# Attention and two expert layers on one core: where the weighted sums of a unit stand among its steps

## The chip, the cores and the metric

The kernel runs on one core of a Trainium2 chip. The metric is the device time of one execution in microseconds (us). The engines are named as in the profile: PE (TensorE, matrix multiplications), PEld (its weight loads), DVE (VectorE), ACT (ScalarE), POOL (GpSimd) and SP (SyncE, which issues the transfers).

## The reference, cut to what matters

```
scores = scale * np.matmul(q, k.transpose(0, 1, 3, 2))        # q, k, v: 4 x 8 x 576 x 64
...
scores = scores + bias.transpose(2, 0, 1)[None, :, :, :]
scores = scores - np.max(scores, axis=-1, keepdims=True)
attn = np.exp(scores)
attn = attn / (np.sum(attn, axis=-1, keepdims=True) + 1e-09)
return np.matmul(attn, v).astype(np.float32)
```

Attention over 4 batches of 8 heads, 576 positions each, 64 wide, with a bias that a small network makes from positions. Behind it come a layer with eight experts, one of which is chosen for each token, and a gated feed-forward layer. The change touches the attention alone, and in it the last line above: the sum of the values weighted by the attention.

## The kernel before, in words

The bias is made first and put into DRAM. Then the attention runs through 16 units; a unit is one batch and one pair of heads (`units`, with index `ui`). A unit has five steps, c = 0 to 4. In steps 0 to 3 the scores of 128 queries against all 576 keys are computed for each of the two heads (`s_pe`, L251); step 4 is the tails' step: the last 64 queries of both heads share the 128 rows. All of it is emitted by one loop over `steps`, whose index is n = 5 ui + c, under a manual schedule: each engine does its instructions in the order in which the code is written.

A step n emits in this order:

- the first half of the transposes of the tile of two steps ago (`t_pe` with i = 0, L274: eight transposes into two PSUM tiles T, four into each), and their copies out of PSUM (`t_ev`, on DVE, L281);
- the scores of the present tile (L251, twelve matmuls of 288 columns with 64 rows each, which run in pairs; in step 4 six with 128 rows);
- the second half of the transposes (ten into two T tiles; two where the old tile is a tails' tile), copied out of PSUM by ACT (L279);
- the weighted sums that stand in this step's list `pe[n]`; in step 1, after the first of them, also the transposes that spread the reciprocals of the row sums (`bc_recip`, L316) and four copies by ACT (L323, L324);
- the bias with the running extremum on DVE (`s_max`, L255), the exponential on ACT (L260), what stands in `ve[n]` on DVE, and loads.

`t_tile` gives out the T tiles from a pool with two buffers:

```
def t_tile():
    return pO.tile([128, 512], F32, tag="T", bufs=2, name="T")
```

A half of the transposes takes both of them. So each half can begin only when the half before it has been copied out of PSUM: the first tile's first transpose after the first copy, the second tile's after the second copy.

The weighted sums of a unit (`pv_list`, L336) are ten blocks: five blocks of keys for queries 0 to 255 (256 columns) and five for queries 256 to 575 (320 columns). A block is two matmuls, one for each head, which the trace shows as four instructions. Five blocks of one kind add up in one PSUM tile `pv` (a pool of two buffers), and one operation on DVE takes it out (L342; at steps 5 ui + 7 and 5 ui + 10). In which step the blocks stand is set by two dictionaries: the key is the step counted from the unit's first, the value is how many blocks.

```
PVA = {4: 1, 5: 2, 6: 2}
PVB = {7: 2, 8: 2, 9: 1}
```

Steps 5 to 9 are steps 0 to 4 of the next unit. So in the steady state there are two blocks in each step, and in the tails' step one of 320 columns of the unit before and one of 256 of the present unit. In step 1 the two blocks stand on either side of the reciprocals' transposes, so there are six groups of blocks between other work in a unit.

What is left of the last unit when the loop ends (`pvq`) is put by hand into the code behind it: `pvs(2)` takes two entries of that list, between the last transposes; the rest goes into the first steps of the expert layer (`at(i, ...)` with 2, 2, 2 and 1 entries).

Of the kernel before, what the change touches and what calls it, by code (L numbers as in the profile page):

```python
# [27 lines left out]

PVA = {4: 1, 5: 2, 6: 2}
PVB = {7: 2, 8: 2, 9: 1}
BL = (20, 28, 30, 32, 36)
VL = (7, 12, 13, 14)
LG = (1, 5, 5, 7, 8, 10, 10)
# [73 lines left out]
def body(tc, qt, kt, va, vb, ws, moe_w_gate, moe_w_output_gate, moe_w1, moe_w2, w_gate, w_val, w_out, ctab, cst, cst2, out):  # L109
    nc = tc.nc  # L110
    with ExitStack() as ctx:
# [153 lines left out]
        def t_pe(E, c, i):  # L265

            t = [t_tile() for _ in range(2)]
            ns = ([128 * n for n in range(4)], [128 * n for n in range(4, 9)])[i] if c < 4 else [128 * n for n in range(4)] if i == 0 else [512]  # L270
            for j, n in enumerate(ns):
                for r in range(2):
                    k, o = slice(64 * r, 64 * r + 64), n + (64 * r if c == 4 and i == 0 else 0)
                    nc.tensor.transpose(t[r][:, 64 * j:64 * j + 64], E[k, o:o + 128], ident[k, k])  # L274
            return t
# [7 lines left out]
        def t_ev(p, b, c, t, i):  # L283

            pt = pts[p, b][c // 2 if c < 4 else 1]
            for r in range(2):
                if c < 4:
                    o, n = 128 * (c % 2) + 64 * r, 4 + i
                    copy(i, pt[:, 4 * i:4 * i + n, o:o + 64], t[r][:, 0:64 * n].rearrange("p (n t) -> p n t", n=n))
                elif i == 0:  # L290
                    copy(i, pt[:, 5 * r:5 * r + 4, 256:320], t[r][:, 0:256].rearrange("p (m t) -> p m t", m=4))
                else:
                    k = slice(64 * r, 64 * r + 64)
                    copy(i, pt[k, 4, 256:320], t[r][k, 0:64])
# [31 lines left out]
        def pv_list(p, b, f):  # L326

            st = {}
            res = []
            w = (256, 320)[f]  # L330
            for c in range(5):
                def m(c=c):
                    if c == 0:
                        st["ps"] = pO.tile([128, 512], F32, tag="pv", bufs=2, name="pv")
                    for hh in range(2):
                        nc.tensor.matmul(st["ps"][64 * hh:64 * hh + 64, 0:w], vt[p][:, hh, b, c, :],  # L336
                                         pts[p, b][f][:, c + (5 * hh if c < 4 else 0), :], start=c == 0, stop=c == 4)
                res.append(m)

            def ev():  # L340
                o = 256 * f
                nc.vector.tensor_tensor(xT[p][:, b * S + o:b * S + o + w], st["ps"][:, 0:w], rbs[p, b][:, o:o + w], ALU.mult)  # L342
            return res, ev
# [491 lines left out]
        pe, ve = {}, {}  # L835
# [6 lines left out]
        for n, (ui, c) in enumerate(steps):  # L842
            p, b = units[ui]
            g = 9 * ui + min(2 * c + 1, 8)
            if c == 0:
# [12 lines left out]
                (m0, e0), (m1, e1) = pv_list(p, b, 0), pv_list(p, b, 1)  # L858
                for ms, q in ((m0, PVA), (m1, PVB)):
                    for k, w in q.items():  # L860
# [96 lines left out]


        pvq = [f for n in sorted(pe) for f in pe[n]]
        pvq = pvq[0:4] + [ve[82][0]] + pvq[4:] + [ve[85][0]]  # L960

        def pvs(n):
            for _ in range(n):
                if pvq:
                    pvq.pop(0)()
# [64 lines left out]
        late.pop()()  # L1030
        for f in lows:
            f()
        pvs(2)
        t_ev(*a[0:3], t_pe(a[3], a[2], 1), 1)
        pvs(2)
        t_ev(*z[0:3], t_pe(z[3], z[2], 0), 0)
# [249 lines left out]
```

## Time and profile before

| | us |
|---|---|
| median of three runs | 1046.68 (1044.06 to 1047.58) |
| the profiled execution, its own time | 1044.97 |
| its span, from the first instruction to the last | 1043.2 |
| PE busy in the span | 1000.8 (96%) |
| DVE, ACT, POOL busy | 577.5, 456.8, 117.1 |

The attention's steps run from 67.7 to about 326 us, the expert layer and the feed-forward layer behind it. In the timeline a row is one or several instructions of one line; where rows of one engine overlap, the engine works on them in a pipeline, so what a group of instructions costs is read from its start to the start of what comes behind it, and not from its own length. A row's bracket says how long the engine was idle ahead of it and whose work ended that.

### The profile page before, as it was taken

How to read it: one execution, taken by the hardware profiler on the slowest of the kernel's cores; microseconds unless marked ns; L12 is line 12 of the kernel's file. 1: busy time of each engine (PE TensorE's matmuls, PEld its weight loads, DVE VectorE, ACT ScalarE, POOL GpSimd, SP SyncE). 2: the span in 40 equal slices, each digit the busy share in tenths (PEclk: the TensorE clock that was granted, in tenths of full speed). 3: DMA queues.
4: the chain of work that ended last, by engine and by line, in shares of the span. 5: the costliest groups of instructions: out<-in, count | busy, mean ns of one | idle time of the engine just before them, and what ended most of it. 6: DMA issues, size and time to landing. Idle time of an engine off the chain costs nothing. (4 is left out here: it accounts for less than half of the span.)

```text
span 1043.2 us, 18947 instructions
## 1 busy us (share of the span) xinstructions
PE 1000.8 (96%) x7525; PEld 797.0 (76%) x7525; DVE 577.5 (55%) x1321; ACT 456.8 (44%) x1027; POOL 117.1 (11%) x117
## 2 busy tenths in 40 slices
PE   6979999999999999999999899999999999999998
PEld 2336666666666899998999677778888888888897
DVE  8966767777766644544566599952223223222322
ACT  6766777777766433332435455431113112211221
POOL 2662332342320000000000000000000000000000
PEclk9997999999999999999999999999999999999999
DMA  6774323333103242633724655511002000200010
GB/s 190 207 258 131 94 84 117 107 105 107 36 3 110 65 163 102 239 118 130 264 102 147 200 175 165 177 51 51 1 1 77 5 1 0 61 1 1 17 25 21
DMA packets 67756, 101.91 MB, mean 98 GB/s; under 512 B 9136, under 2 KB 37936, under 8 KB 67664
## 3 DMA queue, kind: packets, MB, share of 16 engines
q1 hardware_dynamic: 67504, 100.41, 30.3%
q8 instruction: 60, 0.98, 0.4%
q14 instruction: 32, 0.26, 0.1%
q10 hardware_dynamic: 160, 0.26, 0.1%
HBM read 74.63 MB, written 26.03 MB: 96 GB/s over the span
## 5 line engine op out<-in xcount | busy, mean ns | idle before, releaser
L1181 PE MATMUL v<-x,w 128*128 128x512 f32 (+1 forms) x720 | 161.2, 371 | 3.8 <-DVE w L934 3.8
L1181 PE MATMUL g<-x,w 128*128 128x512 f32 (+1 forms) x720 | 158.5, 369 | 1.9 <-ACT x L1136 1.9
L1181 PEld LDWEIGHTS v<-x,w 128*128 128x128 f32 x720 | 125.0, 189 | 31.9 <-DVE w L934 7.5
L1181 PEld LDWEIGHTS g<-x,w 128*128 128x128 f32 x720 | 126.7, 188 | 26.6 <-ACT x L1136 2.1
L1203 PE MATMUL o<-w,uh 128*128 128x512 f32 x432 | 133.4, 390 | 0.0
L1184 DVE TENSOR_TENSOR t<-g,t 128x512 f32<-128x512 f32 (+1 forms) x60 | 38.2, 636 | 168.4 <-ACT t L1183 168.4
L260 ACT ACTIVATE E<-E,st 128x576 f32<-128x576 f32 x144 | 110.6, 774 | 6.4 <-DVE st L255 6.0
L274 PEld LDWEIGHTS T<-ident,E 64*128 64x128 f32 x1312 | 65.6, 141 | 55.5 <-ACT pt L279 27.7
L255 DVE CUSTOM_DVE_ANT_0 E<-S,bias 128x576 f32<-128x576 f32 x128 | 91.9, 755 | 17.9 <-PE S L251 9.4
L1183 ACT ACTIVATE t<-g 128x512 f32<-128x512 f32 (+1 forms) x60 | 33.1, 552 | 153.9 <-PE g L1181 153.9
L336 PE MATMUL pv<-pt,rawv 128*64 128x256 f32 (+1 forms) x640 | 99.3, 423 | 0.0
L1188 ACT ACTIVATE uh<-t 128x512 fp32r<-128x512 f32 (+1 forms) x60 | 35.4, 589 | 145.7 <-DVE t L1185 145.7
L274 PE MATMUL T<-ident,E 64*128 64x64 f32 x1312 | 92.2, 238 | 6.2 <-ACT rb L324 3.6
L1203 PEld LDWEIGHTS o<-w,uh 128*128 128x128 f32 x432 | 80.4, 188 | 16.1
L281 DVE COPY pt<-T 128x256 f32<-128x256 f32 x160 | 59.7, 414 | 54.3 <-PE T L274 54.2
L1203 PE MATMUL o<-w,ul 128*128 128x512 f32 x216 | 84.1, 389 | 0.0
L251 PE MATMUL S<-kh,qz 64*128 64x288 f32 (+1 forms) x576 | 77.6, 320 | 5.2 <-DVE st L255 4.6
L279 ACT ACTIVATE pt<-T 128x320 f32<-128x320 f32 (+1 forms) x160 | 56.0, 391 | 54.5 <-PE T L274 52.4
L545 ACT ACTIVATE qz<-T 128x288 fp32r<-128x288 f32 x63 | 25.8, 410 | 105.6 <-PE T L543 105.5
L546 DVE SCALAR_TENSOR_TENSOR qz<-T,qz 128x288 fp32r<-128x288 f32 x63 | 28.7, 456 | 74.2 <-ACT qz L545 73.7
L1185 DVE TENSOR_TENSOR t<-v,t 128x512 f32<-128x512 f32 (+1 forms) x60 | 38.3, 638 | 54.4 <-PE v L1181 53.1
L251 PEld LDWEIGHTS S<-kh,qz 64*128 64x128 f32 (+1 forms) x576 | 54.8, 192 | 8.0 <-DVE st L255 6.0
(242 smaller groups left out, 1643.9 us busy)
## 6 DMA issues: line engine op xcount, KB each, us to landing
raww<-in_moe_w_dram SPq DMA_DIRECT2D x16, 768.0 KB, 6.1
bscr<-ob SPq DMA_DIRECT2D x36, 288.0 KB, 4.0
bias<-bscr SPq DMA_DIRECT2D x16, 576.0 KB, 5.0
rw<-in_w_gate_dram SPq DMA_DIRECT2D x12, 512.0 KB, 3.8
rw<-in_w_val_dram SPq DMA_DIRECT2D x12, 512.0 KB, 3.6
rw<-in_w_out_dram SPq DMA_DIRECT2D x12, 512.0 KB, 4.0
rawq<-in_qt_dram SPq DMA_DIRECT2D x16, 320.0 KB, 3.8
rawk<-in_kt_dram SPq DMA_DIRECT2D x16, 288.0 KB, 3.2
```

The costliest lines, as they stand in the source:

```text
L251: nc.tensor.matmul(t[:, f, 0:288], x[k, a], y[k, o], start=i == 0, stop=i == 2)
L255: nc.vector.tensor_tensor_reduce(out=E.rearrange("p (a b) -> p a b", a=2), in0=ps[:, :, 0:288], in1=bt[p, hh, c].rearrange("p (a b) -> p a ...
L260: nc.scalar.activation(E, E, AF.Exp, bias=st[:, 2 * c + hh:2 * c + hh + 1], scale=-1.0, accum_out=st[:, 10 + 2 * c + hh:11 + 2 * c + hh])
L274: nc.tensor.transpose(t[r][:, 64 * j:64 * j + 64], E[k, o:o + 128], ident[k, k])
L279: nc.scalar.activation(o, x, AF.Copy)
L281: nc.vector.tensor_copy(o, x)
L336: nc.tensor.matmul(st["ps"][64 * hh:64 * hh + 64, 0:w], vt[p][:, hh, b, c, :], pts[p, b][f][:, c + (5 * hh if c < 4 else 0), :], start=c = ...
L1181: nc.tensor.matmul(t, a[:, 128 * k:128 * k + 128], x, start=k == 0 and n == 0, stop=k == 3 and n == 2)
L1184: nc.vector.tensor_tensor(t, ps[0], t, ALU.mult)
L1185: nc.vector.tensor_tensor(t, ps[1], t, ALU.mult)
L1188: nc.scalar.activation(uh, t, AF.Copy)
L1203: nc.tensor.matmul(ops[j][m], u[:, o], w, start=f == 0 and n == 0, stop=f == NF - 1 and n == 2)
```

## The change

The blocks of 256 columns stand in steps 5 and 6 (three and two), those of 320 in steps 7 and 8 (two and three). The tails' step has none; the step before it and the step behind it have three. The transfers, the number of instructions and their sizes are as before. Behind the loop one more block of the last unit is left over: the list `pvq` begins with five blocks in place of four, and the first `pvs` takes three.

```
-PVA = {4: 1, 5: 2, 6: 2}
-PVB = {7: 2, 8: 2, 9: 1}
+PVA = {5: 3, 6: 2}
+PVB = {7: 2, 8: 3}
...
-        pvq = pvq[0:4] + [ve[82][0]] + pvq[4:] + [ve[85][0]]
+        pvq = pvq[0:5] + [ve[82][0]] + pvq[5:] + [ve[85][0]]
...
-        pvs(2)
+        pvs(3)
         t_ev(*a[0:3], t_pe(a[3], a[2], 1), 1)
         pvs(2)
```

The rows of PE around the tails' step of the kernel before, from the last matmul of its scores to the scores of the next unit's step 0, with the counters that a row waits for (T is a PSUM tile of transposes, E a tile of exponentials, pt their transposes in SBUF, rawv the values; kh and kl are the keys, qz the queries):

```order
L251 MATMUL S<-kl,qz_113 128x288
L274 MATMUL T<-ident,E 128x64 [waits DVE_49] x2
L274 MATMUL T<-ident,E 128x64 x8
L336 MATMUL pv<-pt_995,rawv 64x320 x2
L336 MATMUL pv<-pt_1261,rawv 64x256 x2
L274 MATMUL T<-ident,E 128x64 [waits Activation_49] x2
L274 MATMUL T<-ident,E 128x64 x6
L251 MATMUL S<-kh,qz_115 128x288 [waits Pool_49]
```

The same place in the changed kernel:

```order
L251 MATMUL S<-kl,qz_113 128x288
L274 MATMUL T<-ident,E 128x64 [waits DVE_49] x2
L274 MATMUL T<-ident,E 128x64 x8
L274 MATMUL T<-ident,E 128x64 [waits Activation_49] x2
L274 MATMUL T<-ident,E 128x64 x6
L251 MATMUL S<-kh,qz_115 128x288 [waits Pool_49]
```

The ten transposes of the tails' step and the eight of the next step now stand one behind the other, and the wait for ACT between them has stayed.

PE behind the scores of step 0 in the kernel before, up to the transposes of step 1:

```order
L251 MATMUL S<-kl,qz_115 128x288 x2
L274 MATMUL T<-ident,E 128x64 [waits DVE_49] x2
L274 MATMUL T<-ident,E 128x64 x8
L336 MATMUL pv<-pt_1261,rawv 64x256 x4
L274 MATMUL T<-ident,E 128x64 [waits Activation_49] x2
```

And in the changed kernel:

```order
L251 MATMUL S<-kl,qz_115 128x288 x2
L274 MATMUL T<-ident,E 128x64 [waits DVE_49] x2
L274 MATMUL T<-ident,E 128x64 x8
L336 MATMUL pv<-pt_1258,rawv 64x256 x6
L274 MATMUL T<-ident,E 128x64 [waits Activation_49] x2
```

Step 0 has six matmuls of weighted sums in place of four; in the same way step 3 has six of 320 columns.

## Rows read from the trace of the kernel before

**Rows 1.** The page, parts 1 and 2: busy time of PE; granted clock in 40 slices.
```profile
PE 1000.8 (96%) x7525; PEld 797.0 (76%) x7525; DVE 577.5 (55%) x1321; ACT 456.8 (44%) x1027; POOL 117.1 (11%) x117
PEclk9997999999999999999999999999999999999999
```

**Rows 2.** Windows: stretch, length, busy us of PE, PEld, DVE, ACT, POOL, clock, DMA.
```profile
67.00:92.00 25.00, 18.85 (x187) 14.28 (x179) 11.90 (x34) 13.10 (x32) 5.37 (x9) 0.73 0.50 165
107.50:280.00 172.50, 169.63 (x2077) 114.80 (x2079) 123.61 (x357) 127.00 (x359) 59.63 (x73) 1.00 0.32 98
```

**Rows 3.** Timeline of PE, units 0, 1, 5, 6: start, length, line, operation, count.
```profile
74.54 0.59 PE L274 MATMUL T<-ident,E 64*128 64x64 f32 x10
...
91.85 0.43 PE L274 MATMUL T<-ident,E 64*128 64x64 f32 x2
92.21 0.65 PE L336 MATMUL pv<-pt,rawv 128*64 128x256 f32 x4
...
156.30 0.37 PE L251 MATMUL S<-kh,qz 64*128 64x288 f32 x1
...
157.79 1.30 PE L336 MATMUL pv<-pt,rawv 128*64 128x320 f32 x8
159.02 0.46 PE L274 MATMUL T<-ident,E 64*128 64x64 f32 x8
...
163.38 0.53 PE L274 MATMUL T<-ident,E 64*128 64x64 f32 x10
163.84 1.19 PE L336 MATMUL pv<-pt,rawv 128*64 128x320 f32 x8
164.96 0.46 PE L274 MATMUL T<-ident,E 64*128 64x64 f32 x8
165.23 0.51 PE L251 MATMUL S<-kh,qz 64*128 64x288 f32 x4
...
166.72 1.08 PE L336 MATMUL pv<-pt,rawv 128*64 128x256 f32 x8
167.73 0.46 PE L274 MATMUL T<-ident,E 64*128 64x64 f32 x8
...
168.88 0.51 PE L274 MATMUL T<-ident,E 64*128 64x64 f32 x2
169.32 0.65 PE L336 MATMUL pv<-pt,rawv 128*64 128x256 f32 x4
169.91 0.46 PE L316 MATMUL T<-ident,rw 64*128 64x64 f32 x8
...
171.51 0.40 PE L274 MATMUL T<-ident,E 64*128 64x64 f32 x6 [0.24 <-ACT rb L324]
171.72 0.38 PE L251 MATMUL S<-kh,qz 64*128 64x288 f32 x1
```

**Rows 4.** Timeline of ACT, units 0, 5 and 6.
```profile
75.12 0.77 ACT L279 ACTIVATE pt<-T 128x320 f32<-128x320 f32 x2 [0.42 <-PE T L274]
...
163.94 0.77 ACT L279 ACTIVATE pt<-T 128x320 f32<-128x320 f32 x2 [0.85 <-PE T L274]
...
171.24 0.22 ACT L324 ACTIVATE rb<-T 64x64 f32<-64x64 f32 x1
```

**Rows 5.** Timeline of PEld, unit 0.
```profile
75.60 0.14 PEld L274 LDWEIGHTS T<-ident,E 64*128 64x128 f32 x1 [0.61 <-ACT pt L279]
75.93 0.50 PEld L274 LDWEIGHTS T<-ident,E 64*128 64x128 f32 x7 [0.19 <-ACT pt L279]
```

**Rows 6.** Timeline of DVE, units 5 and 6.
```profile
163.49 0.76 DVE L255 CUSTOM_DVE_ANT_0 E<-S,biast 128x576 f32<-128x576 f32 x1 [0.24 <-PE S L251]
...
165.46 0.76 DVE L281 COPY pt<-T 128x256 f32<-128x256 f32 x2 [1.20 <-PE T L274]
...
168.37 0.70 DVE L281 COPY pt<-T 128x256 f32<-128x256 f32 x2
```

**Rows 7.** Waits of PE from 346 us on, the largest: total, times, longest.
```profile
PE v L1181 <- DVE w L934: 3.8, 8, 0.5
```

## The prediction

> **What bounds the kernel now.** I read the page first: PE is busy for 96% of the span, and its granted clock is full but for one dip [rows 1]. Then the windows: in the steady stretch of the attention PE is busy for 169.63 of 172.50 us at a clock of 1.00, while DVE and ACT work for 123.61 and 127.00 us [rows 2]. So PE is the bound there, and the other two engines count only where PE has to wait for them. The timeline of PE shows where: a unit takes 15.42 us (156.30 to 171.72, step 2 of one unit to step 2 of the next), and the one idle time that the timeline prints in it is 0.24 us ahead of step 2's transposes, ended by ACT [rows 3]. I measured the tails' step of units 1 to 14 in the same way; the time from its ten transposes to the scores of the next unit was 1.84 or 1.85 us in all of them, so one unit stands for the rest.
>
> **What a block costs.** A group of two blocks of 256 columns takes 1.01 us, from its start to the transposes behind it (166.72 to 167.73); a group of one takes 0.59 (169.32 to 169.91) [rows 3]. So a further block costs 0.42 us, and a group costs 0.17 us on top of its blocks. Two blocks of 320 take 1.23 us (157.79 to 159.02), the mixed group of the tails' step 1.12 (163.84 to 164.96) [rows 3]: the wider block costs 0.11 more, 0.53 us. As a cross-check, 0.53 + 0.42 + 0.17 gives the 1.12 of the mixed group.
>
> **What the change adds.** In step 3 a third block of 320 columns, in 15 units (the last one's are outside the loop): 15 x 0.53 = 7.95 us. In step 0 a third block of 256, in 15 units and once more behind the loop: 16 x 0.42 = 6.72 us. Both lie on PE, which is the bound, and nothing there waits that they could hide behind, except at one place (below). Together 14.7 us.
>
> **What it takes away.** In the tails' step PE goes from its ten transposes straight to the eight of the next step. These need the same two T tiles, and ACT must copy them out first. In the kernel before, the blocks cover that: ACT starts its two copies 0.56 us after the ten transposes begin (163.38 to 163.94) and ends at 1.33 us (163.94 + 0.77), while PE comes to the eight transposes at 1.58 us (164.96) [rows 3, 4]. With the blocks gone PE would be there long before ACT is done, and waits. ACT cannot start sooner: it sat idle for 0.85 us until PE was done [rows 4].
>
> Where PE goes on is shown at two places. In unit 0 no blocks stand between the halves: PE's ten transposes begin at 74.54 and ACT's copies at 75.12; the first weight load of the eight comes 0.48 us after ACT's start (75.60), the other seven 0.81 us after it (75.93), each ended by ACT [rows 3 to 5]. At step 1 to 2 of every unit, where one block stands between, ACT's last copy ends at 171.46 (171.24 + 0.22), the transposes go on at 171.51 and the scores follow at 171.72, so 0.26 us after ACT's end [rows 3, 4]. In the tails' step that gives 1.33 + 0.26 = 1.59 us from the ten transposes to the next scores. Before it is 1.85 us (163.38 to 165.23) [rows 3]. So taking 1.12 us of work out brings only 0.26 us; the rest turns into a wait for ACT. Over 16 tails' steps (unit 0's, which holds one block and runs at half clock, and the last one's, which stands behind the loop, taken like the others): 16 x 0.26 = 4.2 us.
>
> Nothing else is late at that place: the scores of step 0 also need the score tile that DVE reads in the tails' step, and DVE is done with it at 163.49 + 0.76 = 164.25, 0.87 us after the ten transposes [rows 6], well ahead of 1.59.
>
> **One small gain.** In step 1 DVE is behind: it starts to copy the T tiles 0.64 us after PE began to fill them (167.73 to 168.37), against 0.50 in step 0 (164.96 to 165.46), because the taking out of the 320 columns and the reciprocals stand ahead of it [rows 3, 6]. PE feels that: from its two transposes to the first block it takes 0.44 us (168.88 to 169.32), but 0.36 in unit 1 (91.85 to 92.21), where that step has no such operation on DVE [rows 3]. The third block in step 0 lets DVE catch up, so 0.08 us come back in 13 units (2 to 14): 1.0 us. The operations that take `pv` out stay where they are, and their sums are ready earlier or at the same time. The SP and POOL queues hold the same instructions in the same order.
>
> **The sum.** 14.7 - 4.2 - 1.0 = +9.5 us, or +0.61 us in a steady unit (15.42 to 16.03). Against the profiled execution's 1044.97 us that is 1054.5; the median of the runs is 1.7 us above that execution, so 1046.68 + 9.5 = 1056.2 us. Does the rest of the kernel absorb it? Behind the attention PE stays the bound: its largest wait from 346 us on is 3.8 us in eight pieces, on DVE [rows 7], which is itself fed by the order of this work and not by a fixed time. So I let it pass in full.
>
> **Bounds.** The scores after the new wait can hardly come before ACT's end plus the first transposes, say 1.45 us, nor later than about 1.75: a saving of 0.40 to 0.10 us a unit, or 6.4 to 1.6 us in all, so +7.3 to +12.1 us. In the dip of the clock (0.73 over 67 to 92 us [rows 2]) PE has one block less to do in unit 0's tails' step; if the full clock came back a step later, that could add up to 3 us, which I take at nothing, because the other rows show full clock through waits of this size.
>
> **The rivals.**
>
> *The group counts, not the wait (faster).* PE pays 0.17 us for each group beyond its blocks, and the change makes one group less in each unit. If the eight transposes could follow the ten without waiting, PE would need 0.46 + 0.27 = 0.73 us there (163.38 to 163.84, 164.96 to 165.23) and not 1.85: 1.12 saved against 0.95 added [rows 3]. Over 16 units that is -2.7, with the 1.0 from step 1 -3.7 us: 1043.0 us. It decides if a T tile is free at that point. Against it: the two tiles are all there are, the order of the changed kernel still shows the wait for ACT, and unit 0 shows the wait itself [rows 5]. 4 in 100.
>
> The Trainium skill has a rule on this side: "TensorEngine Tiling (Array Packing)", section "Key Properties", says that changing the tiling mode, and not merely the tile, drains the engine. The transposes use half the rows and the blocks half the columns, so by that rule fewer changes of kind are a gain. The 0.17 us per group agrees with it, and by that rule alone the time would be the 1043.0 of this rival.
>
> *The wait is worth all of it (slower still).* If PE came to the scores no earlier than before, because the transposes behind the wait run apart rather than close together, the 4.2 us are lost: +13.7, 1060.4 us. For it: in unit 0 the eight weight loads came in two pieces [rows 5]. Against it: behind the same wait in step 2 the scores followed within 0.21 us [rows 3]. 8 in 100.
>
> *A third block is cheaper than the second.* If it cost 0.3 us, since its weights are loaded under the two before it, 31 blocks would give back 3.7 to 4 us: about 1052.5. Against it: the second block of a group, which is under the same cover, costs 0.42. 6 in 100.
>
> *Swallowed later.* A wait behind the attention that ends at a fixed time would take up the delay: 1046.7, no change. The rows show no such wait of this size [rows 7]. 2 in 100.
>
> **How the numbers follow.** My forecast has 80 in 100; its own range is 1053.5 to 1059. Forecast, full wait and cheaper blocks are all slower: 94 in 100. A measurement of this kernel can tell about 0.3%, 3.1 us, from no change. The faster rival lies just beyond that; I put 3 of its 4 on faster and 1 on the same, to which the 2 of the swallowed case come. The range from 1052.5 to 1060.5 takes in the bounds and both rivals on the slow side.
>
> **What would show it.** In the profile of the changed kernel: a unit of 16.03 us (15.9 to 16.2); in the tails' step two rows of transposes with a wait on ACT between them, and the next scores 1.59 us after the ten transposes begin; groups of three blocks that take 1.43 us in step 0 and 1.76 in step 3; 0.36 us from the two transposes to the block in step 1; everything behind the attention shifted by 9 to 10 us. I would be wrong if a unit took 15.42 us or less, which would say that the eight transposes did not wait; or if the units agree and the end does not, which would say that the delay was taken up later.

## The result: 0.9% slower, and the profile after

| | before | after |
|---|---|---|
| median of four runs each | 1046.12 us | 1056.04 us (1053.98 to 1056.99) |
| ratio, after to before | | 1.0093, 95% interval 1.0079 to 1.0107 |
| span of the profiled execution | 1043.2 us | 1052.2 us |

The forecast was 1056.2 us, +9.5 us; measured were +9.9.

The page of the changed kernel, part 1, answers to the first of [rows 1]: PE is busy 2 us more, the span is 9 us longer, and so the share falls from 96 to 95%.

```profile
PE 1002.9 (95%) x7525; PEld 800.0 (76%) x7525; DVE 579.2 (55%) x1321; ACT 457.8 (44%) x1027; POOL 117.2 (11%) x117
```

Busy time, the modelled length of the matmuls, hardly shows a wait. The groups by line show it: ahead of the transposes (L274) PE was idle for 6.2 us before, mostly for the reciprocals' copies (L324), and now for 15.0 us, of which 9.2 are ended by ACT's copies at L279. The first row is of the kernel before (from its page), the other two of the changed one. Columns: line, engine, operation; busy us, mean ns; idle us ahead of it, and what ended it.

```profile
L274 PE MATMUL T<-ident,E 64*128 64x64 f32 x1312 | 92.2, 238 | 6.2 <-ACT rb L324 3.6
```

```profile
L274 PE MATMUL T<-ident,E 64*128 64x64 f32 x1312 | 96.8, 240 | 15.0 <-ACT pt L279 9.2 <-ACT rb L324 3.6 <-DVE lg L383 0.4
L336 PE MATMUL pv<-pt,rawv 128*64 128x256 f32 (+1 forms) x640 | 96.6, 423 | 0.0
```

The timeline of PE of the changed kernel, units 4 to 6, answers to [rows 3]: start, length, line, operation, count.

```profile
159.67 0.38 PE L251 MATMUL S<-kh,qz 64*128 64x288 f32 x1
...
164.16 1.84 PE L336 MATMUL pv<-pt,rawv 128*64 128x320 f32 x12
165.92 0.46 PE L274 MATMUL T<-ident,E 64*128 64x64 f32 x8
...
167.30 0.52 PE L274 MATMUL T<-ident,E 64*128 64x64 f32 x10
168.34 0.73 PE L274 MATMUL T<-ident,E 64*128 64x64 f32 x7 [0.52 <-ACT pt L279]
168.88 0.38 PE L251 MATMUL S<-kh,qz 64*128 64x288 f32 x1
...
169.77 0.68 PE L274 MATMUL T<-ident,E 64*128 64x64 f32 x10
170.38 1.51 PE L336 MATMUL pv<-pt,rawv 128*64 128x256 f32 x12
171.83 0.46 PE L274 MATMUL T<-ident,E 64*128 64x64 f32 x8
...
172.97 0.44 PE L274 MATMUL T<-ident,E 64*128 64x64 f32 x2
173.34 0.65 PE L336 MATMUL pv<-pt,rawv 128*64 128x256 f32 x4
...
175.74 0.38 PE L251 MATMUL S<-kh,qz 64*128 64x288 f32 x1
```

ACT and PEld at the same place answer to [rows 4, 5]:

```profile
167.85 0.77 ACT L279 ACTIVATE pt<-T 128x320 f32<-128x320 f32 x2 [1.37 <-PE T L274]
```

```profile
168.34 0.14 PEld L274 LDWEIGHTS T<-ident,E 64*128 64x128 f32 x1 [0.66 <-ACT pt L279]
168.67 0.26 PEld L274 LDWEIGHTS T<-ident,E 64*128 64x128 f32 x6 [0.19 <-ACT pt L279]
```

What to see: the ten transposes begin at 167.30, ACT starts its copies 0.55 us later, the weight load for the first of the next eight comes 0.49 us after ACT's start (168.34), those for the rest 0.05 us after the second copy's end (167.85 + 0.77 = 168.62, weight loads at 168.67), and the scores follow at 168.88: 1.58 us after 167.30. The groups of three take 1.76 us (164.16 to 165.92) and 1.45 us (170.38 to 171.83). From the two transposes of step 1 to the first block there are 0.37 us. A unit takes 16.07 us (159.67 to 175.74).

DVE at step 1, which answers to [rows 6], now starts its copies 0.49 us after the transposes began (171.83) and has been idle before, so the lateness is gone:

```profile
172.32 0.76 DVE L281 COPY pt<-T 128x256 f32<-128x256 f32 x2 [0.21 <-PE T L274]
```

PE's largest wait behind the attention is the same as in [rows 7]:

```profile
PE v L1181 <- DVE w L934: 3.8, 8, 0.5
```

Where the 9.0 us between the two profiled spans lie can be read from the first score matmul of each tails' step, which in the timeline is the row with 128 rows (128x288). From unit 1 to unit 13:

```profile
100.71 0.53 PE L251 MATMUL S<-kh,qz 128*128 128x288 f32 x2
...
285.80 0.53 PE L251 MATMUL S<-kh,qz 128*128 128x288 f32 x2
```

before, and after:

```profile
102.05 0.53 PE L251 MATMUL S<-kh,qz 128*128 128x288 f32 x2
...
294.85 0.53 PE L251 MATMUL S<-kh,qz 128*128 128x288 f32 x2
```

Read in the same way for the other stretches (two profiles of each kernel; one number where both agree within 0.02 us):

| from tails' step to tails' step | before, us | after, us | difference | forecast |
|---|---|---|---|---|
| unit 0 to 1 | 17.11, 17.06 | 19.61, 18.32 | +1.2 to +2.6 | +0.7 |
| a unit, mean of the twelve from 1 to 13 | 15.42 | 16.07 | +0.64 | +0.61 |
| 13 to 14 | 18.87 | 19.16 | +0.3 | +0.61 |
| 14 to 15 | 17.91 | 18.29 | +0.4 | +0.61 |
| 15 to the first matmul of the expert layer | 5.83 | 6.06 | +0.2 | +0.2 |

The forecast of the first row is the saving of the wait against a block of 256 and one of 320 columns, with no step 1 gain; of the last, a block of 256 against the saving. For the two executions whose spans stand above, the rows add up to +11.1 us (2.5 + 12 x 0.64 + 0.3 + 0.4 + 0.2). The 2.1 us between that and the spans' +9.0 lie ahead of unit 0's tails' step (1.2 us) and behind the attention (1.0 us). Two profiles of the changed kernel differ by 2.1 us in the first of these places and by 1.7 us in the second.

### The profile page after: what moved, and what is told of

The parts are those of the page before. It is cut to its first block, busy times and chain, and to the rows that moved or that the text cites. A ratio compares the mean times of both kernels' runs of the same rounds, so it can differ in the third digit from the quotient of the medians.

```text
span 1052.2 us, 18949 instructions
## 1 busy us (share of the span) xinstructions
PE 1002.9 (95%) x7525; PEld 800.0 (76%) x7525; DVE 579.2 (55%) x1321; ACT 457.8 (44%) x1027; POOL 117.2 (11%) x117
## 5 line engine op out<-in xcount | busy, mean ns | idle before, releaser
L274 PEld LDWEIGHTS T<-ident,E 64*128 64x128 f32 x1312 | 68.9, 142 | 62.1 <-ACT pt L279 22.0
L274 PE MATMUL T<-ident,E 64*128 64x64 f32 x1312 | 96.8, 240 | 15.0 <-ACT pt L279 9.2
L336 PE MATMUL pv<-pt,rawv 128*64 128x256 f32 (+1 forms) x640 | 96.6, 423 | 0.0
L279 ACT ACTIVATE pt<-T 128x320 f32<-128x320 f32 (+1 forms) x160 | 56.1, 392 | 66.7 <-PE T L274 66.0
L546 DVE SCALAR_TENSOR_TENSOR qz<-T,qz 128x288 fp32r<-128x288 f32 x63 | 28.8, 457 | 71.1 <-ACT qz L545 70.7
L251 PEld LDWEIGHTS S<-kh,qz 64*128 64x128 f32 (+1 forms) x576 | 57.1, 194 | 5.8 <-DVE st L255 3.8
```

What stands on the lines that cost most here:

```text
L251: nc.tensor.matmul(t[:, f, 0:288], x[k, a], y[k, o], start=i == 0, stop=i == 2)
L279: nc.scalar.activation(o, x, AF.Copy)
```

## The experiments

Theory: the change moves 0.42 us and 0.53 us of work per unit to places where PE has nothing to hide it behind, and what it frees in the tails' step is taken by a wait for ACT's two copies, because there are only two T tiles. Rival: the wait does not matter, and a moved block costs in proportion to its columns. A second question came from the table's first row: whether the wait in unit 0 also holds the clock down.

**One half: only the block of 256 columns moves (only_256).**

```
-PVA = {4: 1, 5: 2, 6: 2}
+PVA = {5: 3, 6: 2}
 PVB = {7: 2, 8: 2, 9: 1}
```

(and the list behind the loop as in the changed kernel)

> Half of the change: only the block of 256 columns leaves the tails' step (steps 5 and 6 have three and two of them), the block of 320 columns stays there. If the wait for ACT's copies sets the time there, the one block left lies under that wait, the next scores come 1.59 us after the ten transposes as in the changed kernel, and a unit grows by 0.42 - 0.26 - 0.08 = 0.08 us only: about +1.5 us over the kernel before, 1047.6 us; up to 1.7 us more if the full clock comes back late in unit 0, as it did in the profile of the changed kernel. If instead the moved blocks cost by themselves, in proportion to their columns, this half carries 4.4 of the 9.9 us: 1050.5 us.

Measured: 1047.5 us, ratio to the kernel before 1.0018 (1.0003 to 1.0032). PE around the tails' step of unit 5:

```profile
164.85 0.53 PE L274 MATMUL T<-ident,E 64*128 64x64 f32 x10
165.31 0.76 PE L336 MATMUL pv<-pt,rawv 128*64 128x320 f32 x4
166.00 0.63 PE L274 MATMUL T<-ident,E 64*128 64x64 f32 x7
166.44 0.38 PE L251 MATMUL S<-kh,qz 64*128 64x288 f32 x1
...
167.94 1.52 PE L336 MATMUL pv<-pt,rawv 128*64 128x256 f32 x12
```

The block left there does not delay the scores by anything: they come 1.59 us after the ten transposes, as in the changed kernel without any block. A unit takes 15.53 us, +0.10 (0.08 expected). So this half of the change costs little: what the third block charges in step 0 is nearly paid by the 0.26 us of the tails' step and the small gain in step 1.

**The other half: only the block of 320 columns moves (only_320).**

```
 PVA = {4: 1, 5: 2, 6: 2}
-PVB = {7: 2, 8: 2, 9: 1}
+PVB = {7: 2, 8: 3}
```

> The other half: only the block of 320 columns leaves the tails' step (steps 7 and 8 have two and three), the block of 256 stays. By the wait: the next scores again come 1.59 us after the ten transposes, a unit grows by 0.53 - 0.26 = 0.27 us, +4.1 us over the kernel before, 1050.2 us, and unit 0 is as before. In proportion to the columns: +5.5 us, 1051.6 us. The two halves together then make 5.6 us by the wait, well under the 9.9 us of the whole change, and 9.9 us by proportion.

Measured: 1051.6 us, ratio 1.0049 (1.0036 to 1.0062): +5.1 us by the ratio and +5.6 by the medians, with an interval that holds both expectations. So the time does not decide; the trace does: a unit takes 15.71 us, +0.29 (0.27 expected by the wait, 0.35 by proportion), and the scores come 1.59 us after the ten transposes again:

```profile
165.45 0.52 PE L274 MATMUL T<-ident,E 64*128 64x64 f32 x10
165.90 0.65 PE L336 MATMUL pv<-pt,rawv 128*64 128x256 f32 x4
166.50 0.73 PE L274 MATMUL T<-ident,E 64*128 64x64 f32 x7
167.04 0.38 PE L251 MATMUL S<-kh,qz 64*128 64x288 f32 x1
```

The halves make 0.10 + 0.29 = 0.39 us a unit, the whole 0.64. The 0.25 us between them are the saving in the tails' step: either half alone earns it, and the second half earns nothing more. In this kernel's profile one stretch, units 14 to 15, took 20.55 us, with the clock at half for about 7 us; of the other profiles only that of free_tiles has such a dip there, half as long (18.89 us for this stretch), and this execution (1052.14 us) was the longest of its five.

**The wait taken away (free_tiles).** The changed kernel, with the eight transposes of step 0 in the two buffers of `pv`, which are free between step 3 and step 0; to free the second one in time, the sums of 320 columns are taken out two steps sooner (the code behind the loop is fitted to that).

```
-        def t_pe(E, c, i):
+        def t_pe(E, c, i, tag="T"):
...
-            t = [t_tile() for _ in range(2)]
+            t = [pO.tile([128, 512], F32, tag=tag, bufs=2, name="T") for _ in range(2)]
...
-                at_step(ve, 5 * ui + 10, e1)
+                at_step(ve, 5 * ui + 8, e1)
...
-                t_ev(*old[0:3], t_pe(old[3], old[2], 0), 0)
+                t_ev(*old[0:3], t_pe(old[3], old[2], 0, "pv" if old[2] == 3 else "T"), 0)
```

> The changed kernel with the wait taken away: the eight transposes of step 0 go into the two PSUM tiles of the weighted sums, which are free between step 3 and step 0 now that the tails' step has no blocks; for that the 320 columns are taken out by DVE in step 3 in place of step 0. By the wait: PE needs 0.73 us from the ten transposes through the eight, and the second head's scores are held until about 0.92 us, when DVE has read the score tile, so the next scores come 0.75 to 0.95 us after the ten transposes in place of 1.59; 14 times 0.64 to 0.84 us: 1044 to 1047 us. If the wait is not what costs, 1056 us as in the changed kernel.

Measured: 1043.43 us, ratio to the kernel before 0.9974 (0.9964 to 0.9984), 0.6 us below the range expected. The blocks stand where the change put them, and the kernel is 12.6 us faster than the changed one. PE and PEld around the tails' step:

```profile
163.69 0.79 PE L274 MATMUL T<-ident,E 64*128 64x64 f32 x18
164.26 0.88 PE L251 MATMUL S<-kh,qz 64*128 64x288 f32 x4
...
165.39 0.59 PE L274 MATMUL T<-ident,E 64*128 64x64 f32 x10
165.91 1.52 PE L336 MATMUL pv<-pt,rawv 128*64 128x256 f32 x12
167.36 0.46 PE L274 MATMUL T<-ident,E 64*128 64x64 f32 x8
```

```profile
164.23 0.19 PEld L251 LDWEIGHTS S<-kh,qz 64*128 64x128 f32 x1
164.61 0.29 PEld L251 LDWEIGHTS S<-kh,qz 64*128 64x128 f32 x3 [0.19 <-DVE st L255]
```

Eighteen transposes in one row, no wait in it; the first score matmul follows after 0.57 us. What is late next is what was expected: the second head's scores wait for DVE to have read the score tile (164.61, 0.92 us after 163.69). To the ten transposes of step 0 it is 1.70 us, against 2.47 in the changed kernel (167.30 to 169.77), and to the blocks of step 0 it is 2.22 (163.69 to 165.91) against 3.08 (167.30 to 170.38). A unit takes 15.21 us in place of 16.07, so the whole 0.86 us lies in this stretch, and the earlier taking out, the second edit of this run, adds nothing elsewhere. This is the faster rival of the prediction with its condition made true, a T tile free at that point. That rival put the saving at 1.12 us; against the kernel before, the same stretch went from 3.34 us (163.38 to 166.72 [rows 3]) to 2.22, which is just that. The rival forecast 1043.0 us.

**A block where PE waits anyway (step1_third).** The tails' step keeps the block of 320 columns; that of 256 goes to step 1, behind the reciprocals' transposes.

```
-PVA = {4: 1, 5: 2, 6: 2}
+PVA = {5: 2, 6: 3}
 PVB = {7: 2, 8: 2, 9: 1}
```

(and the list behind the loop as in the changed kernel)

> The block of 256 columns goes from the tails' step to step 1, behind the transposes of the reciprocals, where PE waits for ACT anyway: in the kernel before one block ends there at 171.00 and the transposes go on at 171.51. By the same reading the moved block costs nothing there (it ends at 171.42), and the tails' step gives 0.26 us a unit: 16 x 0.26 = 4.2 us less than the kernel before, 1041.9 us, up to 1.7 us more if the clock comes back late in unit 0. If a block costs what it costs wherever it stands: 1046.1 us, no change; if the third block makes something else late in step 1, slower.

Measured: 1043.14 us, ratio to the kernel before 0.9975 (0.9965 to 0.9985). The expectation was 1.2 us lower, within the allowance for the clock.

```profile
170.20 0.46 PE L316 MATMUL T<-ident,rw 64*128 64x64 f32 x8
170.50 0.22 PE L316 MATMUL T<-ident,st 64*128 64x64 f32 x2
170.65 1.08 PE L336 MATMUL pv<-pt,rawv 128*64 128x256 f32 x8
171.67 0.54 PE L274 MATMUL T<-ident,E 64*128 64x64 f32 x7
172.02 0.38 PE L251 MATMUL S<-kh,qz 64*128 64x288 f32 x1
```

From the reciprocals' transposes to the scores of step 2 it is 1.82 us, with two blocks between; before, with one, 1.81 (169.91 to 171.72 [rows 3]). The moved block costs 0.01 us, and the tails' step earns its 0.26: a unit takes 15.17 us, 0.25 less. So here a block has no price of its own; it costs the part of it that does not lie under a wait at its place.

**Both together (step1_free).** The edits of free_tiles on these dictionaries:

```
-PVA = {4: 1, 5: 2, 6: 2}
-PVB = {7: 2, 8: 2, 9: 1}
+PVA = {5: 2, 6: 3}
+PVB = {7: 2, 8: 3}
```

> Both ideas together: no block in the tails' step, the transposes behind it in the free tiles of the weighted sums, and the third block of 256 columns in step 1 behind the reciprocals' transposes in place of step 0. If the moved block is as free in step 1 as the run step1_third showed (the scores of step 2 came 1.82 us after the reciprocals' transposes, against 1.81 in the kernel before), the unit of free_tiles (15.20 us) loses the 0.44 us that the third block costs in step 0: 14.76 us, and 15 times that is 6.6 us off 1043.4: 1036.8 us. If the two gains rest on the same slack, one of them shows alone: 1043 us, as each has by itself.

Measured: 1036.55 us, ratio to the kernel before 0.9917 (0.9900 to 0.9933); a unit takes 14.81 us in the mean (14.77 in most). The two gains add up as expected, and this version is faster than both kernels.

**The clock in unit 0 (unit0_kept, before_look, after_look, unit0_only).** The granted clock falls to the half level (1.2 of 2.4 GHz) in the attention's first steps, between 70 and 77 us, where PE still waits for DVE, and comes back between 86 and 94 us. Unit 0's tails' step lies in the dip. unit0_kept is the changed kernel with one edit, for unit 0 alone; before_look and after_look are the two kernels as they are:

```
-                for ms, q in ((m0, PVA), (m1, PVB)):
+                for ms, q in ((m0, PVA if ui else {4: 1, 5: 2, 6: 2}), (m1, PVB)):
```

> The changed kernel, but unit 0 keeps the order of before (one block in its tails' step). If the new wait in unit 0 is what brings the full clock back later, the clock is back at 88.5 to 90 us as in the kernel before, and the time is about 1.9 us less than the changed kernel's. If the length of the dip changes from run to run anyway, nothing is to be seen beyond the scatter of the runs (3 us).

> The kernel before, once more, to see whether the dip of the clock near 76 to 89 us is the same in another profiled execution. If it hangs on the kernel, it ends at 88.5 to 90 us again; if it varies from run to run, it can be as long as in the changed kernel's profile (to 92 us).

> The changed kernel, once more, for the same question. If the new wait in unit 0 lengthens the dip, it ends near 92 us again; if it varies from run to run, it can end at 88.5 to 90 us. The steady unit should be 16.06 us again, and the wait in each tails' step the same.

The reverse is the kernel before with unit 0's block alone moved:

```
-                for ms, q in ((m0, PVA), (m1, PVB)):
+                for ms, q in ((m0, PVA if ui else {5: 3, 6: 2}), (m1, PVB)):
```

> The kernel before with one block moved, in unit 0 alone: its tails' step gives its one block to step 0, so that the new wait for ACT comes once, in the dip of the clock. If that wait holds the clock down longer, the profile shows a dip of about 20.5 us (as in the four profiles with this wait so far; 13.7 to 17.1 in the six without it), and the time grows by 1 to 2 us. If the length of the dip only varies from run to run, the time grows by 0.2 us, which is not to be seen, and the dip is 13.7 or 17.1 us about as often as 20.5.

The window from 66 to 98 us, columns as in [rows 2], of the kernel before, of its second profile, of the changed kernel, of unit0_kept and of unit0_only:

```profile
66.00:98.00 32.00, 25.61 (x274) 18.35 (x268) 16.07 (x47) 18.39 (x48) 9.84 (x12) 0.79 0.49 154
```

```profile
66.00:98.00 32.00, 26.95 (x278) 19.23 (x270) 16.31 (x46) 18.75 (x48) 9.30 (x11) 0.73 0.48 155
```

```profile
66.00:98.00 32.00, 27.34 (x256) 19.91 (x248) 15.69 (x45) 17.41 (x45) 9.70 (x12) 0.68 0.52 170
```

```profile
66.00:98.00 32.00, 26.89 (x274) 19.30 (x264) 16.27 (x47) 18.27 (x47) 9.86 (x12) 0.73 0.49 157
```

```profile
66.00:98.00 32.00, 26.31 (x254) 19.30 (x246) 14.64 (x41) 16.42 (x43) 9.78 (x12) 0.68 0.48 159
```

The mean clock there is 0.79 or 0.73 without the wait in unit 0, and 0.68 with it. The second profile of the changed kernel, only_256 and step1_third, which have the wait as well, show 20.5 us at half clock in a count of windows of 1 us, as the two kernels with 0.68 here do; all six profiles without it show 13.7 or 17.1.

In before_look (1045.12 us) the full clock came back at 89.1 us, in after_look (1056.47 us, steady unit 16.07) at 91.2, in unit0_kept at 87.9. unit0_kept took 1052.68 us in its one execution, 3.4 us below the changed kernel's median where 1.9 were expected, and 16.85 us from tails' step 0 to 1. unit0_only took 1046.92 us, ratio 1.0015 (1.0002 to 1.0028), and its units 0 to 1 took 19.07 us against 17.1, while every later unit was as before (15.43). So moving unit 0's block costs 1.3 us by the medians and 1.6 by the ratio (0.2 to 2.9) where the terms of a steady unit give 0.2.

That it is the wait that holds the clock down is supported by the two edits, which take it out and put it in alone. The five profiles with the wait also happen to have early dips, which begin at 70.7 to 72.7 us, ahead of the wait; but the two without it whose dips begin at 70.8 and 72.8 us stay at half clock for 17.1 us and not 20.5. The edits move a block's work as well as the wait, so it is not shown that the wait alone does it. How the chip decides is not shown here, and why the dip's start varies, ahead of any difference between the kernels, stays open.

## Why the prediction was right, and where its terms were off

- *What bounds the kernel:* right. The differences measured in the steady units are PE's own work and PE's waits: the blocks, the wait for ACT, and the lateness of DVE in step 1.
- *The third blocks:* 0.53 us in step 3 as forecast (1.76 - 1.23), 0.44 in step 0 in place of 0.42 (1.45 - 1.01).
- *The new wait:* right to 0.01 us. 1.58 to 1.59 us in units 1 to 14, against 1.59 forecast. only_256 and only_320 show that this time is set by ACT's copies and not by what PE does meanwhile, and free_tiles that without them the change would have been a small gain.
- *The gain in step 1:* 0.07 us in place of 0.08, and DVE starts on time there. It came in units 2 to 13; in unit 14 there was nothing to gain, with 0.37 us already before.
- *The sum of a unit:* +0.64 against +0.61.
- *Units 13 to 15:* mis-sized. I took them like the others, and they grew by 0.3 and 0.4 us. The router of the first batch puts its own matmuls there, and before the change PE waited at them, so that the third block of step 0 is partly hidden. In unit 14's step 0 the router's sixteen matmuls took 1.81 us, with 0.50 us in which their weight loads waited for DVE to take out the 320 columns; now they take 1.38, without that wait; in unit 15's step 0 the wait for ACT behind the router's transposes went from 0.68 us to 0.25. The two places before, and after:

```profile
291.13 1.81 PE L371 MATMUL T<-xT,wg 128*32 128x288 f32 x16
...
311.83 0.56 PE L274 MATMUL T<-ident,E 64*128 64x64 f32 x7 [0.68 <-ACT gt L419]
```

```profile
300.36 1.38 PE L371 MATMUL T<-xT,wg 128*32 128x288 f32 x16
...
321.02 0.56 PE L274 MATMUL T<-ident,E 64*128 64x64 f32 x7 [0.25 <-ACT gt L419]
```

- *The clock in unit 0:* taken at nothing, with a bound of 3 us. It was not nothing: moving unit 0's block cost 1.3 to 1.6 us in unit0_only, with a wide interval (0.2 to 2.9). The reason that I gave, that full clock outlasts waits of this size in the steady units, did not hold for a wait inside a dip. This error and that of units 13 to 15 have opposite signs and partly cancel; that the total came within 0.4 us of the forecast is in that part luck.
- *Passing through:* right. Nothing behind the attention took the delay up: from the expert layer's first matmul to the end the two profiles of the kernel before take 714.8 and 714.5 us, those of the changed kernel 713.8 and 715.5.
- *The rivals:* "the group counts, not the wait" was ruled out by the trace of the changed kernel, and free_tiles shows that its price was right (1043.4 us measured, 1043.0 forecast) and its condition what was missing. The rule of the Trainium skill named there ("TensorEngine Tiling (Array Packing)", "Key Properties") agrees with free_tiles, where one group less is a gain (15.42 to 15.21 us a unit); that a drain is what a group costs, no run here shows. "The wait is worth all of it" is ruled out by the 1.59 us, and "a third block is cheaper" by 0.44 and 0.53 us. "Swallowed later" is ruled out by the time itself.

## What to carry to other kernels

Work that stands between two uses of the same two PSUM tiles is cover for their copying out. As long as there are only these two tiles, the copies set the least time of that place, and moving more work out than that only buys a wait. Moving a block is worth what its old place earns less what its new place charges: here one block was free in step 1, where PE waited anyway, and cost 0.44 us in step 0. Where a wait is for a buffer, look for another buffer that is idle at that moment before moving work around it.

## What the runs showed of the hardware

A wait of half a microsecond in a stretch at half clock went with a longer stay there: 20.5 us in five profiles with it, 13.7 or 17.1 us in six without. The same wait at full clock, once in every unit from 1 to 14, left the clock at full in both profiles of the changed kernel. The beginning of the dip varied from 70 to 76 us among profiles, although the program up to there is the same in all of them. Later dips also come in single executions: in only_320's profile the clock was at half for some 7 us in units 14 and 15, and shorter dips between 312 and 348 us stand in those of free_tiles (two), step1_third, unit0_only and after_look.
